# One list of 1788 steps in another order: gated linear attention, then a hard-swish feed-forward, on one core

## The chip, the cores and the metric

The kernel runs on one core of one Trainium2 chip. The metric is the device time of that core in microseconds (us). Before the change the median of three runs is 543.16 us (542.98 to 544.01). A core has a matrix engine (TensorE, PE in the profile, with PEld for its weight loads), a vector engine (VectorE, DVE), a scalar engine (ScalarE, ACT), a general engine (GpSimd, POOL) and a sync engine (SyncE, SP), which here issues all loads and stores. Each engine works through its own queue in the order in which the program gave it instructions.

## The reference

```python
# attention: batch 4, 8 heads, 768 tokens, head size 48
for t in range(S):
    state = alpha[:, :, t, :, None] * state + einsum('bhd,bhe->bhde', k[:, :, t], v[:, :, t])
    y[:, :, t] = einsum('bhd,bhde->bhe', q[:, :, t], state)
# feed-forward on x = y as (3072 tokens, 384)
h = x @ w_in                               # 384 -> 2048
g = h * clip(h + 3.0, 0.0, 6.0) / 6.0
out = g @ w_out                            # 2048 -> 384
```

All inputs come as 64-bit floats[...]; the kernel converts them from their bits.

## The kernel before, in words

The 3072 tokens are 24 tiles of 128 (numbered j); two tiles make a pair g = 0 to 11, and six tiles make one batch entry, where the attention state starts anew. The whole kernel is a set of small functions, one for each kind of step, in a table `steps`. A string lists every step with its numbers, for instance `P.2.3.0`; `run` calls them in that order. The list therefore is the program order on every engine at once: an instruction runs when those ahead of it in its engine's queue have gone and the data and buffers that it needs are ready. The numbers after tile or pair name a bank or a buffer slot.

Steps for one tile of attention:

- `la`, `lk`, `lq`, `lv` load alpha, k, q and v (SP, L251 to L272). From tile 6 on (FIRST = 6) alpha, k and q go into block layouts, whose padding is filled for the first two tiles by a small memset on POOL (L257), issued with the load.
- `ta`, `tk`, `tq` transpose on PE up to tile 5 (L282); from tile 6 on `ca`, `tk`, `tq` are transposes on VectorE (L286). Up to tile 5 `ca` is a ScalarE copy (L300).
- `r` and `p` are two scans on VectorE (L309 with a small reciprocal L313, and L320); `k` and `q` multiply by them (L332).
- `sc`, `u`, `ya`, `yb` are runs of small products on PE (L346 scores, L429 state update, L455 attention output); `m` masks the scores on VectorE (L356); `sm` adds the state (L439), `st` scales it on POOL (L409); `qa`, `sv`, `ck`, `cy` are copies on ScalarE (L366, L419, L378, L464). `cy` gives the feed-forward its input x.
- from tile 8 on `kt`, `kw`, `kr` turn k round by way of DRAM in place of the PE transposes `kb` (L374).

Steps for the weights (16 slices i of 768 KB as they come): `w` loads, `d1`, `d2`, `dx` are ScalarE's part (L186, L196, L191), `d3` VectorE's (two instructions L203, L205 for slices 0, 1, 2, 4; three, L207, L208, L210, for the rest), `d4` an integer add on POOL (L217). Slices 0 to 7 are w_in, 8 to 15 w_out. Raw data stand in three buffers and, for slices 3 and 4, in the part of the second hidden buffer that the steps `fg.1` fill later.

Feed-forward of pairs 0 and 1: `f` (L478), or in halves `fa`, `fb` (L489), is the first layer, `fr` and `fg` its gate (ACT L494, DVE L498); pair 0 has its second layer in `b` (L516). While these use w_in as it is, later pairs use a scheme with fewer multiplications: `y` (25 sums of parts of w_in, made once), `xc` (11 sums of x), 20 products `M` (8 passes, L600), which go out by `n` (ACT copy, L606) and `o` (DVE sums, L537 to L541), then `e` and `h` (gate, L494 and L498). The second layer from pair 1 on is a seven-product scheme: `s` (sums of hidden values, L647 and L664), `P` (16 passes, L703), `K` and `G` (copies and sums of the outputs, L682, L716, L719), `O` (store, L724). `x` are the sums of w_out.

PSUM has eight banks: four for attention, four (m0 to m3) for the feed-forward products, so a product that starts in a bank waits for the last reader of what stood there. `z` (L532) are products with an identity whose results nobody reads; `z.0.8` is eight of them in bank 0.

Of the kernel before, what the change touches and what calls it, by code (L numbers as in the profile page):

```python
# [17 lines left out]
def kernel(  # L18
# [42 lines left out]
    G = 2  # L61
# [510 lines left out]
    for i in range(8):  # L572
        r, o = divmod(i, 3)
        spots.append(raws[r].rearrange("p n w -> p (n w)").bitcast(FP)[:, o * QB : (o + 1) * QB])
    xc = consts.tile([C, len(X_SUMS), C], FP, tag="xc")
# [174 lines left out]
    with tc.manual_schedule():  # L750
        run("""qa.0.0 la.0 z.0.8 ta.0.0 z.0.2 ca.0 lk.0 tk.0.1 la.1 ta.1.2 ca.1 r.0 k.0 kb.0.3 ck.0
               lq.0 tq.0.0 z.0.3 w.2 d1.2 dx.2 p.0 q.0 sc.0.1.2 r.1 m.0 z.0.5 lv.0.0 u.0.3.0 z.0.3
               la.2 ta.2.1 d2.2 ca.2 sv.0.0 lq.1 p.1 tq.1.2 q.1 qa.0.1 qa.1.0 qa.1.1 sm.0.0 lk.1
               tk.1.1 k.1 sc.1.2.3 z.0.1 kb.1.1 r.2 p.2 m.1 sm.0.1 st.1 ck.1 sv.0.1 w.0 d2.0 d1.0
               dx.0 d3.0 d4.0 z.0.2 ya.0.1 yb.0 cy.0 z.0.3 lv.1.1 u.1.2.3 sm.1.0 d3.2 z.0.2 la.3
               lk.2 tk.2.0 k.2 ta.3.2 ca.3 sv.1.0 r.3 d4.2 sm.1.1 st.2 lq.2 tq.2.1 q.2 fa.0.0 sv.1.1
               ya.1.2 kb.2.0 yb.1 sc.2.1.3 w.1 d2.1 d1.1 dx.1 cy.1 fa.2.1 fb.2 d3.1 p.3 m.2 w.3 d2.3
               ck.2 w.5 lk.3 lv.2.2 lq.3 d4.1 w.6 w.7 la.5 fa.1.2 fb.1 lv.3.0 sv.2.0 d2.5 d1.3 d1.5
               fr.0.2.0 d3.3 d3.5 d4.5 u.2.2.0 fb.0 tk.3.1 qa.2.0 fr.0.1.1 ya.2.3 sm.2.0 sm.2.1
               sv.2.1 d4.3 fg.0.2 fg.0.1 st.3 tq.3.2 k.3 q.3 fr.0.0.0 fg.0.0 d2.6 d3.6 f.0.5.3 d1.6  # L760
               d4.6 fr.0.5.1 kb.3.0 ck.3 qa.2.1 sc.3.1.2 m.3 yb.2 d2.7 d3.7 cy.2 qa.3.0 ta.5.0 ca.5
               r.5 sv.3.0 d1.7 d4.7 u.3.1.2 sm.3.0 fg.0.5 f.0.6.1 fr.0.6.0 lk.4 tk.4.3 la.4 ta.4.0
               ca.4 f.0.3.2 sm.3.1 fg.0.6 r.4 st.4 w.9 sv.3.1 d2.9 qa.3.1 ya.3.1 yb.3 cy.3 k.4 p.4
               d1.9 d3.9 d4.9 lq.4 tq.4.2 kb.4.0 f.0.7.0 w.4 d2.4 fr.0.3.1 d3.4 ck.4 f.1.3.3 fg.0.3
               w.8 q.4 sc.4.1.3 p.5 fr.0.7.0 d2.8 d3.8 fg.0.7 d1.4 dx.4 d4.4 d1.8 d4.8 lv.4.1 la.7
               ca.7 u.4.0.2 sm.4.0 m.4 w.12 d2.12 d1.12 d3.12 f.1.0.1 lk.5 d4.12 fr.1.0.1 f.1.7.2
               fr.1.7.0 sv.4.0 fg.1.0 w.10 d2.10 fr.1.3.1 qa.4.0 fg.1.7 tk.5.0 k.5 d1.10 d3.10 d4.10
               la.6 w.11 lk.6 sm.4.1 ca.6 fg.1.3 d2.11 d3.11 d1.11 qa.4.1 d4.11 f.1.6.0 fr.1.6.0
               fg.1.6 tk.6 f.1.1.1 fr.1.1.1 kb.5.1 f.1.5.2 fr.1.5.0 fg.1.5 b.1.0.3 f.1.2.0 w.15
               d2.15 d1.15 lq.5 tq.5.3 r.6 k.6 w.13 lv.5.2 d2.13 fr.1.2.0 d3.15 fg.1.2 d3.13 w.14  # L770
               d1.14 d2.14 lq.6 tq.6 lq.8 fg.1.1 q.5 b.1.1 fa.4.2 ck.5 sv.4.1 fb.4 fr.0.4.0 d1.13
               d4.15 y.3 p.6 y.5 d3.14 fg.0.4 b.0.0.0 b.0.1 sc.5.0.2 u.5.1 st.5 sm.5.0 sv.5.1 m.5
               qa.5.0 qa.5.1 d4.13 lk.8 lv.6.0 sv.6.0 lk.7 q.6 y.6 s.1.1.1 tk.7 f.1.4.1 sv.5.0
               fr.1.4.1 fg.1.4 d4.14 y.10 y.1 x.0 r.7 s.1.0.0 s.1.3.2 y.8 x.1 b.1.2 kb.6.3 ck.6
               P.1.0.2 ya.4.1 ya.5.0 yb.4 yb.5 u.6.2.3 b.0.2 b.1.3 bo.1 cy.4 cy.5 s.1.2.3 x.2 s.1.4
               y.2 k.7 xc.2.1 y.7 p.7 xc.2.3 x.3 xc.2.2 y.9 xc.2.10 y.15 P.1.3.1 K.1.0 P.1.2 K.1.1
               P.1.1.3 G.1.0.0 K.1.2 s.1.5 y.11 P.1.4 G.1.1.1 la.9 la.8 xc.2.4 ca.8 so.1 lq.7 xc.2.5
               y.0 y.4 y.13 P.1.5 b.0.3 bo.0 P.1.6 G.1.3.2 y.12 xc.2.0 y.16 y.17 y.19 y.20 y.18 y.21
               M.2.0.3 qa.6.0 n.2.0.8 xc.2.7 M.2.7.0 n.2.7.9 y.23 xc.2.6 M.2.1 n.2.1.10 sc.6.0.1
               M.2.2 r.8 sm.6.0 tq.7 xc.2.8 qa.6.1 ca.9 q.7 G.1.2.3 la.11 n.2.2.11 sv.6.1 M.2.15.2  # L780
               M.2.16 M.2.3 kb.7.2 M.2.4 n.2.4.12 tk.8 M.2.8 sm.6.1 st.7 m.6 tq.8 o.2.0.0 ya.6.3
               yb.6 sc.7.0.1 M.2.9 xc.2.9 M.2.18.1 o.2.4.0 k.8 y.14 ck.7 qa.7.1 lv.9.1 lv.7.2 sv.7.0
               e.2.0.0 cy.6 qa.7.0 u.7.2.3 o.2.1.0 M.2.10 kt.8 lk.9 n.2.18.13 M.2.17 n.2.10.14
               o.2.6.0 y.22 y.24 sm.7.0 sv.7.1 p.8 h.2.0 M.2.5 M.2.11 n.2.11.15 e.2.4.1 m.7 e.2.1.0
               h.2.1 n.2.5.12 M.2.19 o.2.5.0 M.2.12 n.2.12.11 ya.7.2 yb.7 q.8 o.2.3.0 M.2.6.3 M.2.13
               sc.8.0.1 cy.7 xc.3.1 o.2.3.1 h.2.4 n.2.13.11 o.2.2.0 o.2.7.0 e.2.3.0 o.2.2.1 e.2.2.1
               xc.3.3 sm.7.1 M.2.14 xc.3.4 xc.3.0 xc.3.5 o.2.7.1 P.2.0.1 M.3.0.3 n.3.0.9 xc.3.7
               M.3.7.2 n.3.7.11 h.2.2 xc.3.6 o.2.6.1 h.2.3 xc.3.8 tk.9 e.2.7.1 h.2.7 M.3.1 n.3.1.13
               K.2.0 e.2.6.0 P.2.1.0 M.3.2 kw.8 lv.8.0 O.1.0 O.1.1 la.10 lq.10 lq.9 kr.8 lk.10 O.1.3
               u.8.2.3 ca.10 r.9 qa.8.1 G.2.0.0 k.9 h.2.6 M.3.8 n.3.2.10 e.2.5.1 h.2.5 s.2.0.12  # L790
               s.2.1.15 O.1.2 kt.9 kw.9 M.3.3 M.3.4 n.3.4.8 P.2.3.0 xc.3.9 xc.3.2 o.3.0.0 qa.8.0
               e.3.0.0 M.3.9 M.3.5 s.2.3.14 s.2.2.15 s.2.4 st.8 sv.8.0 K.2.2 o.3.1.0 p.9 xc.3.10
               P.2.2 K.2.1 M.3.10 n.3.10.12 e.3.1.1 s.2.5 P.2.5 tq.9 sm.8.0 sv.8.1 m.8 n.3.5.14 q.9
               qa.9.1 r.10 M.3.11 P.2.4 sm.8.1 h.3.0 st.9 sv.9.0 n.3.11.15 tk.10 G.2.1.1 G.2.2.2
               k.10 kr.9 lq.11 lk.11 sc.9.0.2 m.9 u.9.1.3 h.3.1 sm.9.0 M.3.6.3 kt.10 kw.10 O.2.0
               M.3.12 n.3.12.8 o.3.3.0 ca.11 M.3.18.0 ya.8.0 yb.8 qa.9.0 sv.9.1 n.3.18.10 o.3.6.0
               ya.9.2 yb.9 cy.9 cy.8 M.3.13 n.3.13.8 o.3.3.1 e.3.3.0 o.3.2.0 xc.4.1 o.3.2.1 o.3.7.0
# [135 lines left out]
```

## Time and profile before

| | |
|---|---|
| median of 3 runs | 543.16 us |
| profiled execution: time, span | 543.03 us, 541.3 us |
| PE busy, records | 525.4 us, 6306 |
| VectorE busy | 482.3 us |
| ScalarE busy | 258.5 us |
| POOL busy | 50.1 us |
| HBM read, written | 44.50 MB, 8.91 MB |

The span runs from the first to the last instruction of the profiled execution; its own time lies 1.7 us above. Each fp32 product appears as two records on PE ("passes"); a transpose as one. In the groups "L703 PE" means the matmuls that line 703 of the kernel issues. Busy time of PE is modelled from the starts of the matmuls, so a full row of nines says that no long hole is there, not that a matmul could not be closer to the next.

### The profile page before, as it was taken

Reading aid. Unit: us, or ns where it says so; the run is one execution under the profiler, and the core shown is the slowest. Engines: PE = TensorE matmul, PEld = TensorE weight load, DVE = VectorE, ACT = ScalarE, POOL = GpSimd, SP = SyncE. Lnnn points to the kernel's source line nnn. Section 1 sums busy time; section 2 is a strip of 40 time slices with the busy share of each in tenths; the row PEclk is TensorE's granted clock in tenths of the full one; section 3 lists DMA queues with packets and bytes.
Section 4 is the critical chain, followed back from the end, with each engine's and each line's share of the span. In section 5 each row is a group of like instructions: output and inputs, shape, how many; then the busy total and the mean of one; then the engine's idle time right before and its main releaser. Section 6 shows DMA issues by size and latency. Waiting matters only on the chain.

```text
span 541.3 us, 15109 instructions
## 1 busy us (share of the span) xinstructions
PE 525.4 (97%) x6306; PEld 499.0 (92%) x6306; DVE 482.3 (89%) x849; ACT 258.5 (48%) x503; POOL 50.1 (9%) x71
## 2 busy tenths in 40 slices
PE   8799889899999999999999999999999999999996
PEld 7698767788999999999999999999999999999996
DVE  7999889999999999999999999999999989686381
ACT  4898845311654544453543653643444544443330
POOL 5252424100000000000000000000000000000000
PEclk9999999999999999999999999999999999999999
DMA  9998864410462246355165225352453151000101
GB/s 182 229 245 235 211 208 121 116 42 1 90 157 55 74 104 132 95 124 123 39 149 127 68 69 122 78 136 70 88 127 92 22 127 34 21 9 15 37 9 36
DMA packets 124100, 54.40 MB, mean 101 GB/s; under 512 B 83328, under 2 KB 116864, under 8 KB 124032
## 3 DMA queue, kind: packets, MB, share of 16 engines
q1 hardware_dynamic: 124032, 53.44, 41.4%
q8 instruction: 49, 0.80, 0.6%
q14 instruction: 19, 0.16, 0.1%
HBM read 44.50 MB, written 8.91 MB: 99 GB/s over the span
## 4 chain that ended last, share of the span: by engine, by line
PE 87%; DVE 6%; issue 2%; DMA 2%; ACT 2%; POOL 1%; DVEq 0%; POOLq 0%; ACTq 0%; SPq 0%
PE m_ps L703 36%; PE m_ps L600 34%; PE t_ps L455 4%; PE m_ps L516 3%; PE t_ps L429 2%; PE m_ps L489 2%; PE t_ps L346 2%; PE m_ps L478 1%; PE m_ps L532 1%; POOL w L217 1%; DVE R L309 1%; DMA raw<-in_moe_w_out_dram 1%; DMA kq<-in_k_dram 1%; PE t_ps L282 1%; DVE w L537 0%
## 5 line engine op out<-in xcount | busy, mean ns | idle before, releaser
L703 PE MATMUL m_ps<-w,g_sb 128*128 128x192 f32 x704 | 121.5, 326 | 0.0
L606 ACT COPY g_sb<-m_ps 128x512 f32<-128x512 f32 x110 | 63.8, 584 | 114.9 <-PE m_ps L600 109.4
L703 PEld LDWEIGHTS m_ps<-w,g_sb 128*128 128x128 f32 x704 | 113.8, 190 | 0.3
L703 PE MATMUL m_ps<-rings,g_sb 128*128 128x192 f32 x528 | 91.5, 327 | 0.0
L703 PEld LDWEIGHTS m_ps<-rings,g_sb 128*128 128x128 f32 x528 | 85.4, 190 | 0.4
L600 PE MATMUL m_ps<-xc,w 128*128 128x128 f32 x640 | 84.3, 278 | 0.2 <-DVE xc L537 0.2
L600 PEld LDWEIGHTS m_ps<-xc,w 128*128 128x128 f32 x640 | 78.0, 192 | 1.7 <-issue 0.3
L494 ACT ACTIVATE r<-g_sb,half 128x512 f32<-128x512 f32 x80 | 57.2, 723 | 44.1 <-DVE g_sb L541 18.5
L498 DVE SCALAR_TENSOR_TENSOR g_sb<-r,g_sb 128x512 f32<-128x512 f32 x80 | 53.9, 681 | 2.8 <-ACT r L494 2.2
L600 PE MATMUL m_ps<-xT,raw 128*128 128x128 f32 x400 | 51.6, 276 | 0.1
L600 PEld LDWEIGHTS m_ps<-xT,raw 128*128 128x128 f32 x400 | 48.4, 192 | 0.5 <-ACT g_sb L606 0.2
L409 POOL TENSOR_TENSOR st<-sm,R 128x192 f32<-128x192 f32 x20 | 13.1, 654 | 358.8 <-DVE sm L439 297.7
L647 DVE TENSOR_TENSOR g_sb<-g_sb 128x512 f32<-128x512 f32 (+1 forms) x55 | 42.1, 789 | 3.5 <-PE m_ps L703 3.2
L600 PE MATMUL m_ps<-xT,w 128*128 128x128 f32 x320 | 42.0, 275 | 0.0
L366 ACT COPY A<-q 48x256 f32<-48x256 f32 x88 | 35.4, 403 | 8.9 <-DVE q L332 7.7
L600 PEld LDWEIGHTS m_ps<-xT,w 128*128 128x128 f32 x320 | 39.4, 192 | 0.1
L356 DVE TENSOR_TENSOR A<-t_ps,mask 64x256 f32<-64x256 f32 x96 | 36.0, 413 | 0.5
L478 PE MATMUL m_ps<-xT,w 128*128 128x256 f32 x144 | 33.1, 382 | 1.1 <-DVE g_sb L498 1.1
L537 DVE TENSOR_TENSOR g_sb<-g_sb 128x512 f32<-128x512 f32 x40 | 27.2, 691 | 6.9 <-ACT g_sb L606 6.2
L309 DVE TENSOR_TENSOR_SCAN R<-t,ones 128x516 f32<-128x516 f32 x24 | 30.4, 1265 | 2.6 <-ACT t L300 2.6
L600 PE MATMUL m_ps<-xc,raw 128*128 128x128 f32 x240 | 32.0, 276 | 0.0
L478 PEld LDWEIGHTS m_ps<-xT,w 128*128 128x128 f32 x144 | 26.6, 190 | 5.2 <-DVE g_sb L498 1.8
(104 smaller groups left out, 735.5 us busy)
## 6 DMA issues: line engine op xcount, KB each, us to landing
raw<-in_moe_w_out_dram SPq DMA_DIRECT2D x8, 768.0 KB, 4.5
raw<-in_moe_w_in_dram SPq DMA_DIRECT2D x6, 768.0 KB, 6.7
v<-in_v_dram SPq DMA_DIRECT2D x48, 96.0 KB, 3.2
out_dram<-oh SPq DMA_DIRECT2D x44, 96.0 KB, 1.8
far<-kq SPq DMA_DIRECT2D x64, 64.0 KB, 2.2
kb<-far SPq DMA_DIRECT2D x64, 64.0 KB, 2.0
aq<-in_alpha_dram SPq DMA_DIRECT2D x36, 96.0 KB, 2.5
kq<-in_k_dram SPq DMA_DIRECT2D x36, 96.0 KB, 2.6
```

The costliest lines, as they stand in the source:

```text
L309: nc.vector.tensor_tensor_scan(out=reverse(R, n - 1, n), data0=reverse(ax, n, n), data1=reverse(ones, n, n), initial=0.0, op0=ALU.mult, op ...
L356: nc.vector.tensor_tensor(out=to[:, a], in0=sc[a][half], in1=mask[half, half].unsqueeze(1).to_broadcast([HB, NP, HB]), op=ALU.mult)
L366: nc.scalar.copy(out=to[:, a], in_=Q_t[j][64 * a : 64 * a + D, :, half])
L455: nc.tensor.matmul(y_of(j, (i + 1) // 2, p)[:, HB * b : HB * b + HB], vb[:, p, e : e + 32], A_t[j][:, b, 2 * p + a], start=(b == 0 and i = ...
L478: nc.tensor.matmul(h[:, f], w1[:, kk, o : o + C], xT_t[g][:, kk], start=(kk == 0), stop=(kk == KT - 1))
L494: nc.scalar.activation(out=to, in_=h, func=AF.Relu, bias=half, scale=1.0 / 6.0)
L498: nc.vector.scalar_tensor_tensor(out=to, in0=r, scalar=1.0, in1=h, op0=ALU.min, op1=ALU.mult)
L537: eng.tensor_tensor(out=out, in0=in0, in1=in1, op=ALU.add if s1 > 0 else ALU.subtract)
L600: nc.tensor.matmul(acc[g][i][:, f * C : (f + 1) * C], spots[w][:, f * C : (f + 1) * C], x_of(g, x), start=(first and f == 0), stop=last, s ...
L606: nc.scalar.copy(out=slots[z], in_=acc[g][i])
L647: nc.vector.tensor_tensor(out=out, in0=in0, in1=in1, op=ALU.subtract)
L703: nc.tensor.matmul(to[g], a, rhs[:, f], start=(first and f == 0), stop=(last and f == HF - 1), skip_group_check=True)
```

## The change

The string is replaced by another order of the same steps. No function changes, and the number of steps of each kind for each tile, pair and slice is the same, 1788 in all. What differs is where each step stands, and which bank or slot it uses; the `z` steps are still 29 products in sum, of which three now stand in pair 2's part. Among pair 0's half steps, `fa` and `fb` keep their work and change banks. The core of the diff, with the places that the prediction speaks of:

```diff
-        run("""qa.0.0 la.0 z.0.8 ta.0.0 z.0.2 ca.0 lk.0 tk.0.1 la.1 ta.1.2 ca.1 r.0 k.0 kb.0.3 ck.0
-               lq.0 tq.0.0 z.0.3 w.2 d1.2 dx.2 p.0 q.0 sc.0.1.2 r.1 m.0 z.0.5 lv.0.0 u.0.3.0 z.0.3
...
-               ya.1.2 kb.2.0 yb.1 sc.2.1.3 w.1 d2.1 d1.1 dx.1 cy.1 fa.2.1 fb.2 d3.1 p.3 m.2 w.3 d2.3
...
-               w.8 q.4 sc.4.1.3 p.5 fr.0.7.0 d2.8 d3.8 fg.0.7 d1.4 dx.4 d4.4 d1.8 d4.8 lv.4.1 la.7
-               ca.7 u.4.0.2 sm.4.0 m.4 w.12 d2.12 d1.12 d3.12 f.1.0.1 lk.5 d4.12 fr.1.0.1 f.1.7.2
-               fr.1.7.0 sv.4.0 fg.1.0 w.10 d2.10 fr.1.3.1 qa.4.0 fg.1.7 tk.5.0 k.5 d1.10 d3.10 d4.10
-               la.6 w.11 lk.6 sm.4.1 ca.6 fg.1.3 d2.11 d3.11 d1.11 qa.4.1 d4.11 f.1.6.0 fr.1.6.0
-               fg.1.6 tk.6 f.1.1.1 fr.1.1.1 kb.5.1 f.1.5.2 fr.1.5.0 fg.1.5 b.1.0.3 f.1.2.0 w.15
...
-               M.2.0.3 qa.6.0 n.2.0.8 xc.2.7 M.2.7.0 n.2.7.9 y.23 xc.2.6 M.2.1 n.2.1.10 sc.6.0.1
...
-               P.11.1.3 K.11.2 K.11.1 P.11.4 s.11.5 P.11.5 O.9.2 so.0 O.9.3 G.11.1.1 O.11.1 P.11.6
-               G.11.3.2 O.11.3 O.10.3 G.11.2.0 O.11.2 G.11.0.1 O.11.0""")
+        run("""z.0.5 z.0.3 z.0.1 z.0.8 qa.0.0 w.0 d2.0 d3.0 la.0 ta.0.0 ca.0 r.0 lk.0 tk.0.1 k.0
+               z.0.2 p.0 la.1 ta.1.2 lq.0 tq.0.3 ca.1 r.1 lk.1 lv.0.0 sv.0.0 d1.0 kb.0.0 ck.0 z.0.2
+               u.0.2.1 sm.0.0 sv.0.1 q.0 qa.0.1 tk.1.0 k.1 p.1 z.0.2 sc.0.2.3 m.0 la.2 ta.2.0 ca.2
+               dx.0 w.2 d2.2 kb.1.0 ck.1 lq.1 r.2 sm.0.1 st.1 tq.1.2 q.1 d3.2 z.0.3 d1.2 dx.2 lv.1.1
...
+               qa.1.0 d2.3 ya.1.2 yb.1 cy.1 fa.1.2 lq.3 ck.2 d1.3 p.3 d3.3 lv.2.2 u.2.3.2 sm.2.0
+               d4.3 fb.2 tq.3.1 q.3 fb.1 qa.2.0 sm.2.1 sv.2.0 st.3 fr.0.2.0 fg.0.2 lk.4 tk.4.0
...
+               fr.0.6.1 yb.2 cy.2 w.9 d2.9 q.4 qa.4.1 d1.4 d1.9 dx.4 la.6 w.8 d3.4 r.5 lk.5 w.10
+               d3.9 p.5 ca.6 fg.0.6 d4.9 w.12 lq.5 lv.4.1 d2.8 d3.8 f.0.7.2 d1.8 st.4 d4.8 d4.4 w.11
+               fr.0.7.0 fg.0.7 f.1.7.0 fr.1.7.1 fg.1.7 sc.4.0.2 m.4 f.1.1.1 fr.1.1.0 fg.1.1 f.1.3.3
+               fr.1.3.1 d2.10 d1.10 tk.5.3 f.1.0.2 d2.12 d3.10 d4.10 w.13 fg.1.3 fr.1.0.0 fg.1.0 k.5
...
+               d4.13 sc.5.0.3 yb.4 f.1.5.0 fr.1.5.1 fg.1.5 tk.6 m.5 b.1.0.2 fb.4 b.1.1 d1.15 d4.15
+               st.5 y.5 w.14 la.7 lk.7 cy.4 d2.14 qa.5.1 ck.5 b.0.0.1 fr.0.4.0 d3.14 k.6 q.6 ca.7
...
+               y.19 xc.2.6 sm.6.0 G.1.2.2 y.20 M.2.0.2 lv.12.1 la.8 O.1.1 O.1.0 ca.8 y.18 y.21 y.23
...
+               st.7 lk.8 O.1.3 lq.8 lk.9 la.9 la.10 tk.8 tq.8 lq.10 lq.9 ya.6.1 yb.6 M.2.9 z.1.3
...
+               e.11.2.0 h.11.2 s.11.4 e.11.3.1 h.11.3 P.11.1.0 s.11.5 G.11.0.1 O.11.0 O.10.3 K.11.1
+               P.11.4 G.11.1.2 P.11.5 G.11.2.1 O.11.2 P.11.6 G.11.3.0 O.11.3 O.9.2 O.11.1""")
```

## The prediction

> **What bounds the kernel now.** I read the page first, then busy time by stage, then the waits, then the order of time at the places that the new order changes.
>
> ```profile
> span 541.3 us, 15109 instructions
> PE 525.4 (97%) x6306; PEld 499.0 (92%) x6306; DVE 482.3 (89%) x849; ACT 258.5 (48%) x503; POOL 50.1 (9%) x71
> PE   8799889899999999999999999999999999999996
> DMA  9998864410462246355165225352453151000101
> ```
>
> TensorE is busy nearly throughout; only the first ten slices (13.5 us each) and the last show holes. Loads fill the DMA engines in the first five slices. By stage (columns: stretch, its length, then busy us and instructions of each engine, clock, DMA share, GB/s):
>
> ```profile
> 0.00:27.00 27.00, 21.42 (x310) 19.10 (x310) 22.41 (x42) 17.27 (x27) 10.91 (x23) 1.00 1.03 206
> 27.00:54.00 27.00, 26.51 (x458) 23.16 (x457) 26.28 (x44) 23.91 (x41) 11.10 (x9) 1.00 0.93 239
> 54.00:81.00 27.00, 23.16 (x163) 18.43 (x162) 23.31 (x34) 17.84 (x27) 9.15 (x12) 1.00 0.77 211
> 81.00:108.00 27.00, 25.73 (x307) 19.80 (x307) 26.65 (x38) 12.13 (x22) 7.88 (x12) 1.00 0.47 119
> 108.00:135.00 27.00, 26.64 (x150) 23.19 (x149) 26.01 (x42) 3.98 (x10) 0.00 (x0) 1.00 0.08 22
> 135.00:459.00 324.00, 323.90 (x4215) 318.13 (x4214) 310.16 (x568) 155.64 (x324) 11.01 (x17) 1.00 0.41 96
> 459.00:541.30 82.30, 77.98 (x713) 77.18 (x711) 47.44 (x87) 27.73 (x55) 0.00 (x0) 0.99 0.07 21
> ```
>
> From 135 us on PE idles 0.1 us in 324. VectorE is close behind (310 of 324, 13.8 idle): two engines run neck and neck, and a product often starts 0.1 to 0.5 us after the vector result that it needs. So the time is PE's fixed work, plus its stalls up to 132 us (where M.2.0, the first fast product, starts), plus the tail. In starts of neighbouring matmuls, taking the commonest distance of each kind as its rate, PE loses 17.0 us before M.2.0 and 2.9 after. What ends waits there:
>
> ```profile
> DVE t L286 <- POOL aq L257: 3.2, 2, 1.8
> PEld t_ps L282 <- DVE s L439: 2.3, 2, 2.0
> PEld m_ps L478 <- DVE g_sb L498: 1.8, 2, 1.5
> ```
>
> The first is the root of the others: VectorE's transposes of alpha for tiles 7 and 6 (ca.7, ca.6) waited 1.42 and 1.75 us for a small fill on POOL that stood in POOL's queue behind the weight adds d4.8 and d4.10. Behind each transpose in VectorE's queue stood results that PE needed (sm.4.0, fg.1.3). A second loss is in the same stage, VectorE beside POOL:
>
> ```profile
> 61.21 2.49 DVE L210 SCALAR_TENSOR_TENSOR raw<-raw,w 128x768 uint32<-128x768 uint32 x1
> 69.64 0.96 DVE L210 SCALAR_TENSOR_TENSOR raw<-raw,w 128x768 uint32<-128x768 uint32 x1
> 60.68 2.20 POOL L217 TENSOR_TENSOR w<-w,g_sb 128x768 int32<-128x768 int32 x1 [3.56 <-ACT g_sb L191]
> ```
>
> The same instruction takes 0.96 us alone and 2.49 beside a POOL add.
>
> **What the Trainium skill says.** TensorE: Matmul & The Clock Gate, section "Architectural detail": the vector, scalar and POOL queues are strict FIFO, and only TensorE may pull a weight load ahead. The trace agrees: the fills above waited for their turn. The same page, Part 3, "The mechanism": a weight load overlaps a running matmul only where its row group differs. That fits the stops below. GPSIMD Engine Reference, section 1: POOL shares its SBUF interfaces with VectorE; the 2.49 against 0.96 us is that. DMA: Bandwidth & Descriptors, "Issuing engines are not separate DMA queues": all loads share 16 engines; here landings before 45 us follow each other at some 1.15 us per 192 KB tile and 2.0 to 2.3 us per weight slice.
>
> **The change, part by part.** No step is added or dropped; both orders hold 1788 steps, the same products and the same 29 idle ones (58 records). Only places, banks and slots move, so the costs are in stalls.
>
> *Stops of small-product runs.* In order of time on PE:
>
> ```profile
> 152.68 1.16 PE L600 MATMUL m_ps<-xc,w 128*128 128x128 f32 x8
> 153.68 1.06 PE L600 MATMUL m_ps<-xc,raw 128*128 128x128 f32 x8
> 154.66 0.69 PE L346 MATMUL t_ps<-q,k 48*64 48x64 f32 x32
> 155.41 1.16 PE L600 MATMUL m_ps<-xc,w 128*128 128x128 f32 x8
> ```
>
> A pass of L600 normally starts 0.112 us after the last. Into a small run it takes 0.205, out of it 0.149 where a small pass takes 0.007, and one load later costs 0.101: 0.093+0.142+0.101 = 0.34 us per run. Counting the two orders, 45 runs become 43, and changes of kind inside runs go from 51 to 53 at 0.03 each: -0.68+0.06 = **-0.6 us**.
>
> *Tail.* After PE's last product:
>
> ```profile
> 537.02 0.32 ACT L716 COPY oh<-m_ps 128x192 f32<-128x192 f32 x1 [10.08 <-PE m_ps L703]
> 537.36 1.77 SPq L724 DMA_DIRECT2D out_dram<-oh  x4
> ```
>
> SP issues four stores behind the last copy, 0.47 us apart (O.11.3, O.10.3, O.11.2, O.11.0). The new order leaves three (O.11.3, O.9.2, O.11.1). The end follows the last issue, so **-0.5 us**.
>
> *The start.* SP's first load is now weight slice 0, then alpha, k, alpha, q. Alpha of tile 0 landed at 4.0 us; one slice ahead of it makes that about 6.2. PE first does 17 idle products (34 records; at the cold 0.213 us until 6.6 us, then 0.112) to about 7.8, so the first scan r.0 moves from 6.75 to about 9.1. Meanwhile VectorE converts slice 0 (d3.0, 1.3 us), formerly done at 21 us. VectorE loses 2.3-1.3 = 1.0, and gains 0.4 where q.1 used to wait for its load: **+0.5 us** on VectorE. If the slice comes too late to be that cover, it is +2.3. Behind the new first load stand all the other loads; by my count of landings la.5 comes at 41.9, as before (41.8).
>
> *The two fills.* la.6 now stands before d4.9 in the list, so its fill follows d4.7 on POOL, with ca.6 some 9 us of vector work behind d3.7. la.7's fill follows d4.15 and st.5, with 8 us of vector work from d3.15 to ca.7. Both waits should go: -3.2 us on VectorE. SP must have passed w.9 for la.6 and w.14 for la.7, by my walk at 47 and 82 us, 10 us or more before they are needed. VectorE's waits for G.1.0 and G.1.1 (0.8 together) go too, since these now stand later than their products: -0.8. Sum on VectorE: -3.2-0.8+0.5 = **-3.5 us**. The overlap of vector conversions with POOL adds also changes; it stretched VectorE by some 6 us in all (means against commonest distances on L203 to L210 and the scans). I take no change, with -2 and +2 as ends.
>
> *What of this reaches PE.* For each product I sum PE's work ahead of it and VectorE's work up to the result it needs, at the commonest distances (scan 1.26+0.10, second scan 1.14, multiply 0.60, mask 4 x 0.36, transpose 0.96, xc sum 0.22; PE: M 0.90, P 2.60, f 2.60). The difference is the lead; PE's stalls must be at least VectorE's lateness minus the lead. Before, the least leads are 1.9 (f.1.1.1), 2.5 (b.1.0), 3.9 (M.2.7: 116.5-112.6), 4.1 (P.2.3: 151.8-147.7). These are the very places where PE waited or had no slack. After: 1.1 (f.1.3), 1.5 (f.1.0), 2.9 (b.1.0), 4.5 (M.2.1: 117.2-112.7), 3.6 (P.2.3: 150.3-146.7). VectorE's lateness at P.2.3 was 21.3 and becomes 21.3-3.5 = 17.8, so PE's stalls there can fall from 16.9 to 17.8-3.6 = 14.2: -2.7. My walk along PE itself (loads, conversions, then banks freed by fg steps) puts M.2.0 at 127.9 instead of 131.9, -4.0, so P.2.3 binds. Later the least lead at tile pair 8 falls from 20.0 to 17.6 (P.8.1). Without recovery only -0.9 would be left; VectorE has 13.8 us of idle in 135 to 459 to recover from, so I give back 0.5: **-2.2 us**. The three idle products now in M.2 are inside these sums.
>
> Sum: -0.6-0.5-2.2 = -3.3. The profiled execution took 543.03 (1.7 around its span), so 539.7; the median of the runs shown is 0.1 higher, giving **539.8**.
>
> **Rivals.** *Gain lost in the middle*: VectorE, at 96% there, can't recover, or its conversions overlap POOL more (+2), and PE stalls in M.2 to P.8. What is left is stops and tail, -1.1: 542.1. For it: the smaller leads at P.2.3 and P.8.1. Against: the 13.8 us of idle. *Late start carried through* (slower): ScalarE is 24 of 27 us busy in 27 to 54. The 2.3 us of the first alpha would then pass unabsorbed through its queue, and cy.1, which lets fb.2 start, stands behind more copies (29.8 becomes 31.3 by my walk, +1.5). That gives 3.8-1.1 = +2.7: 545.9. It decides once more than 2.2 us of the delay reaches M.2.0. Against: the same walk has PE at f.0.3 at 39.0 with as much work behind it (29.5 us) as before at f.0.5. *All of the opening*: VectorE's -3.5 and better overlap (-2) reach PE, so -5.5-0.6-0.5 gives 536.6. Against: P.2.3's lead. That the order is changed but not the critical queue is ruled out for the fills, which do move.
>
> **How the numbers follow.** Forecast 0.48 (own range 538.5 to 541.2); gain lost 0.17, half of it within 0.2% (1.1 us, about what a measurement can tell); late start 0.22, nearly all of it slower; whole opening 0.08; other gains lost by a single new wait of about 1 us 0.05. Faster 0.48+0.08+0.08+0.05 = 0.69, same 0.10, slower 0.21. The range 537.2 to 545.2 leaves about one in ten on each side.
>
> **What would show it.** No wait of DVE L286 on POOL; r.0 at 9 us; M.2.0 at 128 to 129 us; three stores after the last copy; 43 small runs; PE without a wait over 0.5 us at P.2.3. Wrong if ScalarE's cy.1 comes after 33 us, if f.1.x waits for banks in sum more than 4 us, or if PE stops behind vector sums at pair 8.

## The result, and the profile after

The kernel after takes 536.38 us (median of 4 executions, 536.24 to 537.02), the kernel before 543.20 (4 executions, 542.98 to 544.01): a ratio of 0.9874, 95% interval 0.9857 to 0.9891, 6.8 us less. The forecast was 539.8 with a range of 537.2 to 545.2. It had the sign right and the time just outside its range, at the fast end: 3.4 us less were forecast, twice as much came. M.2.0, foretold for 128 to 129 us, starts at 125.70. The profiled execution took 536.33 us with a span of 534.5.

Where the two traces part can be read from three marks:

| | before | after | difference |
|---|---|---|---|
| start of M.2.0, the first fast product | 131.88 us | 125.70 us | -6.18 |
| from there to the last matmul's start | 404.78 | 404.71 | -0.07 |
| from there to the end of the span | 4.59 | 4.12 | -0.48 |

So nearly all of it lies ahead of M.2.0. The page of the kernel after, in the lines that answer to those shown of before:

```profile
span 534.5 us, 15145 instructions
PE 524.2 (98%) x6306; PEld 498.9 (93%) x6306; DVE 477.1 (89%) x849; ACT 257.6 (48%) x503; POOL 50.4 (9%) x71
PE   7799999999999999999999999999999999999997
DMA  9998877006615155254354455055364042100001
```

VectorE was busy 482.3 us and now is 477.1, with the same 849 instructions: some of them take less time. By stage (stretch, its length, then busy us and instructions of PE, PE's loads, VectorE, ScalarE and POOL, granted clock, DMA share, GB/s):

```profile
27.00:54.00 27.00, 26.77 (x437) 23.95 (x434) 26.44 (x44) 24.96 (x49) 8.94 (x9) 1.00 0.98 259
54.00:81.00 27.00, 27.00 (x282) 23.26 (x281) 25.08 (x41) 20.45 (x31) 10.91 (x9) 1.00 0.77 204
81.00:108.00 27.00, 27.00 (x187) 19.23 (x186) 26.73 (x35) 9.96 (x21) 7.48 (x14) 1.00 0.37 86
135.00:459.00 324.00, 324.00 (x4173) 318.48 (x4172) 308.93 (x565) 152.60 (x319) 10.19 (x17) 1.00 0.41 95
```

In 54 to 108 us PE was busy 48.89 of 54 us; now it is busy 54.00. In starts of neighbouring matmuls, counted as in the prediction, PE loses 10.15 us up to 45 us in the kernel before and 10.10 in the kernel after, so nothing is gained up to there; up to M.2.0 it loses 17.00 and 10.84. What the change gains ahead of M.2.0 is gained between 45 us and M.2.0. VectorE's waits in the first 135 us:

```profile
DVE w L203 <- ACT w L196: 2.4, 1, 2.4
DVE s L439 <- PE t_ps L429: 1.3, 1, 1.3
DVE half L80 <- PEq L915: 0.8, 1, 0.8
```

The line with L286 behind POOL, 3.2 us before, is gone from this list. The first of these is the new start: VectorE waits for the first weight slice. Conversions beside POOL adds, from the order of time:

```profile
59.62 0.69 DVE L207 TENSOR_SCALAR w<-w 128x768 f32<-128x768 f32 x1
60.95 0.96 DVE L210 SCALAR_TENSOR_TENSOR raw<-raw,w 128x768 uint32<-128x768 uint32 x1
...
81.70 2.03 POOL L217 TENSOR_TENSOR w<-raw 128x768 int32<-128x768 int32 x1 [0.17 <-POOL kq L257]
82.38 1.77 DVE L207 TENSOR_SCALAR w<-w 128x768 f32<-128x768 f32 x1
92.69 1.96 DVE L332 TENSOR_TENSOR q<-q,P 128x512 f32<-128x512 f32 x1
```

The same L207 takes 0.69 or 1.77 us. Against the lower quartile of each form, instructions stretched in this way before 132 us lost 5.9 us in the kernel before and 3.8 in the kernel after. At the end:

```profile
530.77 0.32 ACT L716 COPY oh<-m_ps 128x192 f32<-128x192 f32 x1 [10.08 <-PE m_ps L703]
528.61 3.79 SPq L724 DMA_DIRECT2D out_dram<-oh  x4
```

Three of these four stores stand behind the last copy, as forecast.

### The profile page after: what moved, and what is told of

It reads as the page before. It is cut to its first block, busy times and chain, and to the rows that moved or that the text cites. A ratio compares the mean times of both kernels' runs of the same rounds, so it can differ in the third digit from the quotient of the medians.

```text
span 534.5 us, 15145 instructions
## 1 busy us (share of the span) xinstructions
PE 524.2 (98%) x6306; PEld 498.9 (93%) x6306; DVE 477.1 (89%) x849; ACT 257.6 (48%) x503; POOL 50.4 (9%) x71
## 4 chain that ended last, share of the span: by engine, by line
PE 88%; DVE 6%; POOL 2%; ACT 1%; DMA 1%; issue 0%; SPq 0%; DVEq 0%; POOLq 0%
PE m_ps L703 34%; PE m_ps L600 34%; PE m_ps L478 6%; PE t_ps L455 4%; PE t_ps L346 2%; PE t_ps L429 2%; PE m_ps L489 2%; DMA v<-in_v_dram 1%; PE m_ps L516 1%; DVE rings L647 1%; PE t_ps L282 1%; DVE raw L537 1%; ACT raw L191 1%; DVE g_sb L647 1%; DVE w L537 1%; POOL v L96 1%
## 5 line engine op out<-in xcount | busy, mean ns | idle before, releaser
L600 PE MATMUL m_ps<-xc,w 128*128 128x128 f32 x640 | 82.7, 277 | 0.3 <-DVE w L541 0.3
L600 PEld LDWEIGHTS m_ps<-xc,w 128*128 128x128 f32 x640 | 77.5, 192 | 1.5 <-issue 0.5
L600 PE MATMUL m_ps<-xT,raw 128*128 128x128 f32 x400 | 52.5, 277 | 0.0
L600 PEld LDWEIGHTS m_ps<-xT,raw 128*128 128x128 f32 x400 | 48.6, 192 | 0.6
L600 PE MATMUL m_ps<-xT,w 128*128 128x128 f32 x320 | 42.0, 276 | 0.0
L600 PEld LDWEIGHTS m_ps<-xT,w 128*128 128x128 f32 x320 | 39.3, 192 | 0.1
L600 PE MATMUL m_ps<-xc,raw 128*128 128x128 f32 x240 | 31.8, 276 | 0.0
L600 PEld LDWEIGHTS m_ps<-xc,raw 128*128 128x128 f32 x240 | 29.6, 192 | 0.1
```

Of the source, the lines that this page charges most:

```text
L600: nc.tensor.matmul(acc[g][i][:, f * C : (f + 1) * C], spots[w][:, f * C : (f + 1) * C], x_of(g, x), start=(first and f == 0), stop=last, s ...
```

## The experiments

Two theories stood at first. A: PE's stalls before M.2.0 follow VectorE's lateness, which two things make: the waits for the alpha fills, and instructions that take longer beside a POOL add (their stretch). B: they follow the order and the banks of PE's own products, and VectorE is not the cause. A third cause came to light on the way and is told with its runs. The kernels for these runs are those of before or after with the one edit shown. The runs share the busy time of 62 to 108 us as a measure (columns as above), here before and after:

```profile
62.00:108.00 46.00, 40.96 (x374) 31.47 (x374) 42.19 (x62) 22.82 (x39) 14.19 (x22) 1.00 0.58 160
```

```profile
62.00:108.00 46.00, 46.00 (x402) 35.69 (x401) 44.04 (x64) 23.41 (x41) 15.75 (x20) 1.00 0.56 142
```

### The fills, in both directions

In the kernel before, the fills of alpha tiles 6 and 7 were taken out of the load and issued on POOL ahead of d4.6:

```diff
-        if j < FIRST + NQ:
+        if j < FIRST + NQ and name != "a":
...
+    def pad_a(j):
+        for o in (BLK, 3 * BLK):
+            nc.gpsimd.memset(quads["a", j % NQ][o : o + BLK, :, V - 1, D - BLK : BLK], 1.0)
...
-  d2.6 d3.6 f.0.5.3 d1.6 d4.6
+  d2.6 d3.6 f.0.5.3 d1.6 pa.7 pa.6 d4.6
```

> The kernel before with one edit: the two small POOL fills for alpha of tiles 7 and 6 are issued ahead of the weight add d4.6 instead of behind d4.8 and d4.10; everything else keeps its place. Theory A (the opening was lost by VectorE being late, and these fills are the largest part): the two waits of 3.2 us are gone from VectorE, PE's stalls before M.2.0 fall from 17.0 to some 14, time 540.2 (539.5 to 541). Theory B (the places of the first-layer products and their banks decide, the fills are hidden behind them): 542.5 to 543.4.

Measured: 539.85 us (5 executions, 539.44 to 540.14), ratio 0.9942 (0.9922 to 0.9961) against 542.87. M.2.0 starts at 128.62 us, 3.26 earlier; no wait of L286 on POOL is left.

```profile
62.00:108.00 46.00, 43.71 (x390) 33.71 (x389) 45.25 (x66) 22.81 (x39) 14.07 (x18) 1.00 0.59 161
```

PE's busy time in the stage grows by 2.75 us without any product of PE having been moved. The reverse, in the kernel after: the same fills put behind POOL adds, with the transposes right behind them.

```diff
-  d3.14 k.6 q.6 ca.7 fg.0.4 d1.14 d4.14
+  d1.14 d3.14 d4.14 pa.7 ca.7 k.6 q.6 fg.0.4
...
-  d3.9 p.5 ca.6 fg.0.6
+  d3.9 p.5 fg.0.6
...
-  st.4 d4.8 d4.4
+  st.4 d4.8 pa.6 ca.6 d4.4
```

> The changed kernel with the fills put back behind weight adds: fill of tile 6 behind d4.8 with its transpose ca.6 right behind d3.8, fill of tile 7 behind d4.14 with ca.7 right behind d3.14, which makes VectorE wait as in the kernel before. Theory A: VectorE waits some 1.9 and 1.8 us for POOL; 1.3 of it takes the place of its wait for the tile-4 state update at 70 us, the rest reaches PE: 538.0 (537.2 to 539). Theory B: below 536.9.

Measured (one execution): 538.79 us, span 537.0, M.2.0 at 127.97. The wait is back, and PE's stalls with it:

```profile
DVE t L290 <- POOL aq L267: 4.1, 2, 2.1
```

```profile
62.00:108.00 46.00, 44.37 (x376) 34.27 (x377) 41.32 (x63) 22.51 (x39) 15.47 (x22) 1.00 0.55 141
```

(L290 is line 286 of the kernel after, moved by the added lines.) VectorE waits 4.1 us, of which 2.27 reach M.2.0. B, which had the fills without influence, falls as the only cause.

### The POOL adds cut to 8 columns, in both kernels

This leaves out the low bits of the weights, and with them nearly all of POOL's work in this stage; everything else keeps its place.

```diff
-        nc.gpsimd.tensor_tensor(out=dst.bitcast(I32), in0=high.bitcast(I32),
-                                in1=lo.bitcast(I32), op=ALU.add)
+        nc.gpsimd.tensor_tensor(out=dst[:, 0:1, 0:8].bitcast(I32),
+                                in0=high[:, 0:1, 0:8].bitcast(I32),
+                                in1=lo[:, 0:1, 0:8].bitcast(I32), op=ALU.add)
```

> The kernel before with POOL's weight adds d4 cut to 8 columns of each slice, so the low weight bits are left out for the rest: POOL is nearly free, so neither the overlap with VectorE (5.9 us of stretched vector instructions before 135 us) nor the fills' wait (3.2 us) is left. Theory A: nearly all of the opening's difference goes, about 537.0 (536 to 538.5). Theory B: the order of the products still costs, 540 or more.

> The changed kernel with the same cut adds (low weight bits left out). Its VectorE is stretched by 3.8 us in the opening, but PE has no stall from 45 us to M.2.0, so little can be gained there. Theory A: 535.8 (535.2 to 536.4), so that the difference to the kernel before with cut adds is 1 to 2 us, of which 0.5 tail and 0.6 stops. Theory B: the difference stays at 4 us or more.

Measured (one execution each): before 538.01 us, M.2.0 at 126.84; after 535.73, M.2.0 at 125.55.

```profile
62.00:108.00 46.00, 45.08 (x395) 34.95 (x394) 44.72 (x67) 22.44 (x39) 6.26 (x20) 1.00 0.58 153
```

```profile
62.00:108.00 46.00, 46.00 (x401) 35.63 (x400) 42.92 (x66) 23.15 (x41) 4.94 (x18) 1.00 0.51 126
```

With the adds out of the way the two kernels are 2.3 us apart instead of 6.8; theory A had expected 1 to 2. The times of these single executions need care. In that of the kernel before the granted clock was 0.5 from 18.1 to 21.5 us, and it stands 0.24 us behind the one with early fills at 41 us, where both have issued the same products. By stage, with the clock as the third column from the right:

```profile
15.00:20.00 5.00, 3.13 (x45) 2.86 (x46) 3.56 (x7) 2.09 (x6) 0.00 (x0) 0.81 0.93 157
20.00:25.00 5.00, 5.00 (x117) 4.34 (x116) 4.63 (x11) 4.89 (x7) 0.54 (x2) 0.85 1.01 310
```

So the comparison is taken from 41 us to M.2.0: 87.89 us with early fills, 85.87 with small adds, which is 2.02 less. VectorE's instructions that are stretched by over 0.2 us lose 5.2 us before 132 us with early fills and 0.5 with small adds. In the kernel after, the small adds bring 0.15 at M.2.0, 0.14 of it ahead of 41 us: what stretch is left there is covered. Between the two kernels 1.3 us remain at M.2.0 (126.84 against 125.55), which neither the fills nor POOL explain.

### What remains: a stop inside a run of small products

Lengths of runs and places in them are counted here in passes, from 0; a product is two passes. (The expectations call a pass a product: their runs of 128 and 160 are passes too.)

In the trace of the kernel with small adds PE stands still once in that stage, inside a run of small products, for 1.13 us. The kernel before has the same stop. It was in its list of waits, and the prediction passed it over:

```profile
PE t_ps L429 <- issue: 1.4, 1, 1.4
```

```profile
104.15 1.99 PE L455 MATMUL t_ps<-A,v 128*32 128x64 f32 x128
106.07 0.66 PE L429 MATMUL t_ps<-v,kb 64*64 64x48 f32 x26
108.18 0.33 PE L429 MATMUL t_ps<-v,kb 64*64 64x48 f32 x6 [1.44 <-issue]
108.43 1.88 PE L516 MATMUL m_ps<-w,g_sb 128*128 128x384 f32 x5
```

"issue" is time in which the engine waits for nothing that the profile shows. The run ya.4 ya.5 yb.4 yb.5 u.6 has 160 passes, the only one so long; it stops behind pass 153, and 1.66 us lie between the starts of this pass and the next, where 0.015 is usual. The longest run of the new order has 128. So a theory Q: a long run stops PE. Its first run, with VectorE's sums moved behind the update that they read:

```diff
-  u.13.0.2 sc.13.1.3 M.5.12 P.4.4
+  sc.13.1.3 M.5.12 P.4.4
...
-  ya.12.3 yb.12 cy.12 yb.13 cy.13
+  ya.12.3 yb.12 cy.12 yb.13 u.13.0.2 sm.13.0 cy.13
...
-  ya.14.2 yb.14 sv.15.1 yb.15 cy.15
+  ya.14.2 yb.14 sv.15.1 yb.15 u.15.0.3 sm.15.0 sm.15.1 cy.15
```

> The kernel after with the state updates u.13 and u.15 (and the VectorE sums that read them) moved from ahead of two large products to the end of the run of small products that follows, so that two runs of 128 become runs of 160; the number of runs stays 43. Theory Q (a run of small products longer than some 150 stops PE for over 1 us, wherever it stands): at about the 154th product of each of the two runs PE stops for 1.1 to 1.7 us without a wait that the profile shows; time 536.4 + 2 x 1.1 to 1.7 = 538.6 to 539.8. Rival L (the stop in the kernel before belongs to its place: loads, or a wait for an operand): no such stop, 536.2 to 536.8.

Measured: 539.6 us (538.64 to 539.61, 3 executions). In this kernel the copies sv.13.1 and sv.15.1 take the half state before its sum, so that part of the attention result is of an older state; instructions and sizes are the same. Of the two runs of 160 only u.13's stopped, behind its pass 150 and for 1.18 us; u.15's did not. A miss for both sides: the stop can be made anew, but length alone does not make it.

The same run cut in the kernel before, by moving u.6 behind the next large product, once with the small adds, once with the early fills, and once with nothing else:

```diff
-  yb.4 yb.5 u.6.2.3 b.0.2 b.1.3
+  yb.4 yb.5 b.0.2 u.6.2.3 b.1.3
```

> The kernel before with the POOL adds of the weights cut to 8 columns, as in the run with small adds (the conversion of the weights is left incomplete by it), and with the one run of 160 small products cut into 128 and 32 by the large product behind it (b.0.2). Theory Q: the stop of 1.13 us at 102 us goes, a further run costs 0.34: M.2.0 at 126.1 instead of 126.8, time 537.2. Rival L: the stop stays at u.6, M.2.0 at 126.8 to 127.2, time 538.0 to 538.4.

> The kernel before with the two fills of alpha early, as in the first experiment, and with the run of 160 small products cut by b.0.2. Theory Q, with PE not held by VectorE any more: 539.85 - 1.2 + 0.34 = 539.0, M.2.0 at 127.8. If VectorE's lateness holds PE there instead (it was 3.6 us less covered before), the stop goes but another wait takes its place: 539.6 to 539.9.

> The kernel before with its one run of 160 small products cut into 128 and 32 by the large product behind it, and nothing else. Theory Q: the stop of 1.66 us inside the run goes and a further run costs 0.34. If that reaches the end beside the fills' waits: M.2.0 at 130.6, time 541.9. If VectorE's lateness (21.3 us at P.2.3, stalls 17.0, lead used 4.3 of about 5) holds PE instead: at most 0.7 of it is left, 542.5 or more. Rival L: the stop stays, 543.2.

Measured. With small adds: 535.49 us (2 executions), M.2.0 at 124.22, the stop gone, PE busy 46.00 of 46. M.2.0 is 2.62 us earlier than without the cut, which is more than Q expected. But 1.59 of it stand before 41 us, where the two programs are alike: the execution without the cut is the one with the clock of 0.5 from 18.1 to 21.5 us. From 41 us to M.2.0 it is 1.0 us, near the 0.8 forecast. With adds and stop gone, and the fills' waits down to 0.6 us, the kernel before is at 535.49 us and the kernel after with small adds (one execution) at 535.73: nothing of the 6.8 us is left. With early fills: 538.61 us (11 executions, 537.32 to 541.33), M.2.0 at 127.50, 1.12 earlier than with the fills alone. With nothing else: 541.94 us (20 executions, 541.58 to 542.98), ratio 0.9984 (0.9977 to 0.9991), M.2.0 at 130.32, 1.57 earlier. The stop goes in all three. In the kernel before it had not reached the end in full: of the 1.57 us, 0.34 are lost again behind M.2.0 (405.12 us to the last matmul's start instead of 404.78, with the wait of L600 for xc grown from 0.2 to 0.5 us), and the medians differ by 0.95.

The first two of these three also measure the stretch a second time: with early fills and the run cut it is 86.77 us from 41 us to M.2.0, with small adds and the run cut 84.84, which is 1.93 less. So from 41 us to M.2.0 the runs of the kernel before bring 3.26 by the fills, 1.12 by the cut and 1.93 by the adds, 6.3 us in all; the kernel after gains 6.1 between 45 us and M.2.0, and cutting its adds brings 0.01 there. (Up to 41 us the execution with small adds and the cut is 1.35 us ahead of the one with early fills and the cut. Of this 0.5 stand ahead of any add; whether the rest is the adds' is open.)

Length or place? Six long runs at once (four of 160, two of 144 passes), made as above in the kernel after, with other slots where a run's own stand in the way:

> The kernel after with the state updates u.9, u.13, u.15, u.17, u.19 and u.23 (and the VectorE sums that read them) moved to the end of the run of small products that follows: four runs of 160 and two of 144 in place of six of 128. Some copies of the state then come before the sum that they should follow, so the attention result is of an older state; the instructions and their sizes are the same. Theory Q in the form that the runs so far leave (a run that passes some 150 small products is liable to stop PE for over 1 us, not every time): stops of about 1.1 us without a shown wait in at least two of the four runs of 160, near product 150; none in the two of 144 or in the remaining runs of 128. Rival L (the stop is tied to its place in the program): only u.13 stops again.

Measured: 539.3 us (538.99 to 539.5, 3 executions). Only u.13's run stopped, behind pass 150 again (1.41 us):

```profile
264.69 1.99 PE L455 MATMUL t_ps<-A,v 128*32 128x64 f32 x128
266.61 0.56 PE L429 MATMUL t_ps<-v,kb 64*64 64x48 f32 x23
268.36 0.34 PE L429 MATMUL t_ps<-v,kb 64*64 64x48 f32 x9 [1.19 <-issue]
```

Q as I had it falls, and rival L, "the place decides", took this run. What is there at the place? In the two traces a transfer of one kind alone runs during the stop, here in the kernel before, 104 to 109 us:

```profile
q8 instruction: 1, 0.02, 1.8%
```

Over the whole kernel this queue carries 49 packets of 16 KB, 0.80 MB. By their number these are PE's own instructions. The Trainium skill, Runtime: NRT & Kernel Launch, section "Instruction fetch mechanics", says that instructions come in blocks of 16 KiB, 256 instructions, and that crossing a block is "mostly hidden". The trace agrees on the blocks: 6306 passes with a load each over 49 blocks are 129 passes per block. It shows a case that is not hidden. The middle half of the fetches in the kernel before come 98 to 149 passes after the one ahead. Around the stop the distances are 200 and 75: one fetch, at 105.39 us, comes about 80 passes late (at 0.015 us each, some 1.2 us), and its packet ends at 106.81; PE stops at 106.5 and goes on at 108.2. The same pair is there at u.13's run (199 and 86). In all six stopped runs of the traces PE goes on 1.25 to 1.48 us after the end of such a packet.

A late fetch alone does not stop PE: in the kernel before the fetches at 188.06 and 478.54 us, beside runs of 128, come 191 and 218 passes after the one ahead, and nothing stops. Theory F: a run of small products goes through a whole block in 2 us; where a block begins early enough in the run to be used up inside it, PE stands before the next one. By my count back from the fetches, that means a beginning in the first 17 or so of 160 passes, so that a run of 128 can't stop at all. Two runs test it by leaving out eight idle products at the very start, which shifts every block by 16 passes against runs that are not touched:

```diff
-        run("""z.0.5 z.0.3 z.0.1 z.0.8 qa.0.0 w.0
+        run("""z.0.5 z.0.3 z.0.1 qa.0.0 w.0
```

> The kernel with six long runs of small products once more, with eight idle products fewer at its very start, which moves every later instruction of PE 16 records nearer to the front of its stream. (As before, some copies of the state come before the sum that they should follow.) Theory F (PE's instructions come in blocks of 16 KB; a run stops where it uses up a whole block before the next has come, which needs a block to begin in the first 17 or so of its 160 products; in the run before this, blocks begin at product 7 of u.13's run, which stopped at 150, and 6 and 5 products ahead of u.15's and u.19's runs, which did not): all blocks begin 16 products later, so u.13's run stops no more, and u.15's and u.19's runs stop at about product 153, for 1.1 to 1.7 us each. Rival L (the stop belongs to u.13's place or operands): u.13's run stops again, u.15's and u.19's don't.

> The kernel before with eight idle products fewer at its very start, and nothing else. Theory F: the block that began at product 10 of the run of 160 now begins at 26, so that the run ends before it is used up: the stop of 1.66 us goes, no further run is made, M.2.0 at about 130.2, time 541.5 to 542.0. Rival L: the stop stays, M.2.0 at 131.9, time 543.0 to 543.4.

Measured, six long runs (539.96 us, 2 executions): u.13's run no longer stops (0.45 us are left in the large product behind it), and u.19's, which had not stopped before, stops behind pass 151 for 1.85 us. u.15's run, for which I had expected a stop too, has none.

```profile
264.65 1.99 PE L455 MATMUL t_ps<-A,v 128*32 128x64 f32 x128
266.57 0.68 PE L429 MATMUL t_ps<-v,kb 64*64 64x48 f32 x32
...
384.50 1.99 PE L455 MATMUL t_ps<-A,v 128*32 128x64 f32 x128
386.42 0.56 PE L429 MATMUL t_ps<-v,kb 64*64 64x48 f32 x24
388.62 0.33 PE L429 MATMUL t_ps<-v,kb 64*64 64x48 f32 x8 [1.64 <-issue]
```

The kernel before with the same shift: 541.68 us (12 executions, 541.04 to 542.76), ratio 0.9978 (0.9969 to 0.9986), M.2.0 at 129.90, 1.98 earlier. Of this 0.62 stand ahead of 41 us already, where PE has eight products less to do. Its run of 160 stands uncut and no longer stops:

```profile
103.58 1.99 PE L455 MATMUL t_ps<-A,v 128*32 128x64 f32 x128
105.50 0.68 PE L429 MATMUL t_ps<-v,kb 64*64 64x48 f32 x32
```

F holds in three of its four points (before, u.13, u.19) and L falls. A count that needs no fetch says the same: from PE's first pass on, u.13's stop is ahead of pass 3265 in both kernels with long runs, and with eight products left out the 0.45 us in the large product are ahead of pass 3265 too, 16 passes further on in the program. The stop keeps its place in PE's stream, not in the list of steps. At u.15's run the fetch came with pass 9 of the run and was in time; at u.19's it came with pass 126. Why one fetch comes so much later than another stays open, and with it the fourth point.

### The terms of the sum, one by one

The tail. In the kernel after, O.11.1 was moved ahead of O.11.2 and O.9.2 ahead of O.11.0:

```diff
-  G.11.0.1 O.11.0 O.10.3 K.11.1 P.11.4 G.11.1.2 P.11.5 G.11.2.1 O.11.2 P.11.6 G.11.3.0 O.11.3 O.9.2 O.11.1
+  G.11.0.1 O.9.2 O.11.0 O.10.3 K.11.1 P.11.4 G.11.1.2 P.11.5 G.11.2.1 O.11.1 O.11.2 P.11.6 G.11.3.0 O.11.3
```

> The kernel after with two of its last three stores (O.11.1 and O.9.2) issued before O.11.2 and O.11.0, so that only one store is left behind the last copy. Theory A (the end follows the last issue on SP, 0.47 us per store): span shorter by 0.94 us, 533.6, and a time of 535.4. Rival T (the end follows the last store's landing, however many stand before it): span 534.5, time 536.4 as it was.

Measured: 535.28 us (535.20 to 535.36), span 533.6. The span is 0.93 us shorter. SP issues two stores in this last stretch where there were four:

```profile
528.64 2.83 SPq L724 DMA_DIRECT2D out_dram<-oh  x2
```

The price of 0.47 us per store behind the last copy is right, and rival T falls.

The start:

```diff
-        run("""z.0.5 z.0.3 z.0.1 z.0.8 qa.0.0 w.0 d2.0 d3.0 la.0 ta.0.0 ca.0 r.0 lk.0 tk.0.1 k.0
-               z.0.2 p.0 la.1 ta.1.2 lq.0 tq.0.3 ca.1 r.1
+        run("""qa.0.0 la.0 z.0.8 ta.0.0 ca.0 r.0 lk.0 tk.0.1 k.0
+               z.0.2 p.0 la.1 ta.1.2 lq.0 w.0 tq.0.3 ca.1 r.1 d2.0 d3.0
```

> The kernel after with alpha, k, alpha and q loaded ahead of weight slice 0, as before, and with slice 0's conversion moved behind r.1; nine idle products are spread over the first gaps as before. It tests the term 'start' of the sum. Theory A (VectorE's work ahead of M.2.0 sets PE, and the new start costs it 0.5 us): M.2.0 comes 0 to 0.8 us earlier, time 535.6 to 536.4. Rival S (the new start is itself a part of the unforeseen gain, slice 0 being converted while VectorE has nothing else): M.2.0 at least 1 us later, time 537.4 or more.

Measured: 535.96 us (535.82 to 536.11), M.2.0 at 125.27, 0.43 earlier. So the new start costs what was put down for it (0.5); other moves ahead of 45 us have made up for it, since PE's loss up to there is the same in both kernels.

The idle products in pair 2:

```diff
-  M.2.9 z.1.3 M.2.18.1
+  M.2.9 M.2.18.1
```

> The kernel after without the three idle products that stand behind M.2.9 (0.67 us of PE; they compute nothing that is used). If PE's own work sets the time from M.2.0 on: -0.67 us, 535.7. If VectorE's lead at the products that follow (M.2.14, P.2.3) is used up, so that the idle products only fill a wait: 0, 536.4, with a new PE stall of 0.4 to 0.7 us there. Theory A holds VectorE 15.9 us late at P.2.3 against stalls of 10.9 and a lead of 3.6, so it expects most of it lost: 536.1 (535.7 to 536.4).

Measured: 536.50 us (536.27 to 536.74), span 534.5: nothing is gained, where theory A had expected 0.3. PE has a new wait at that very place, for VectorE's sum:

```profile
138.50 0.68 DVE L541 SCALAR_TENSOR_TENSOR g_sb<-m_ps,g_sb 128x512 f32<-128x512 f32 x1
139.23 0.60 PE L600 MATMUL m_ps<-xc,w 128*128 128x128 f32 x3 [0.41 <-DVE g_sb L541]
```

In the kernel after the three idle products stand there instead:

```profile
137.80 0.83 PE L532 MATMUL m_ps<-ident 128*128 128x128 f32 x6
```

The stops at the edges of small runs: eleven large products moved into runs, of the kind

```diff
-  kw.14 kr.14 u.14.1.2 M.6.3 M.6.4
+  M.6.3 kw.14 kr.14 u.14.1.2 M.6.4
```

(that is, M.6.3 now stands between sc.14 and u.14).

> The kernel after with eleven of its runs of small products cut in two by a large product that stood beside them, so that 43 runs become 54 and changes of kind inside runs fall by 11. By the terms of the sum, 11 x (0.34 - 0.03) = 3.4 us: 539.8, all of it in PE after 135 us and none of it before (M.2.0 at 125.7). Rival: VectorE, close behind PE there, sets the time as much as PE does and the stops are hidden in its waits: under 1 us, 537.0 or less.

Measured: 540.40 us (540.09 to 541.24, 6 executions). In the profiled execution PE's clock was 0.96 in the first 45 us, which puts M.2.0 at 126.44; from there to the last matmul's start it takes 408.51 instead of 404.71, 3.8 us for eleven runs, or 0.35 per run net (the changes of kind inside runs fell from 25 to 6 there; with 0.03 for each, 0.40). So PE sets the time over this stretch, though not at every place (at 139 us it was VectorE, as shown above), and the price of 0.34 was, if anything, a little low.

### A version that beats both

The two edits that helped, the start and the tail, together:

> The kernel after with both edits that helped alone: the attention loads ahead of weight slice 0, and one store instead of three behind the last copy. If their gains add: -0.4 at M.2.0 (125.3) and -0.94 at the end, span 533.1, time 534.9 to 535.1. If the two share a cause they would not add: 535.3 or more. Against the kernel before: ratio 0.985 to 0.9855.

Measured: 534.90 us (5 executions, 534.82 to 535.16), ratio to the kernel before 0.9836 (0.9812 to 0.9861). The gains add, and this is the fastest version that was run.

## Why the prediction was right in its sign and wrong in its size

**Right.** No wait of L286 on POOL; r.0 at 8.7 us (9 foretold); three stores behind the last copy, -0.5; the start +0.5 (measured +0.43; its own parts, 1.0 less 0.4, make 0.6); from 135 us on PE's fixed work (no wait of PE beyond a few tenths); the fills' term itself, 3.2 on VectorE, of which the run with early fills alone brought 3.26 at M.2.0. None of the three signs of a wrong prediction came: cy.1 stood at 31.9 us, no product of f.1 waited for a bank, PE did not stop at pair 8. What happened is nearest to the rival called "all of the opening" (536.6), which I gave 0.08. That its number is met within 0.2 us is in part luck: it has 5.5 us from the fills, the G waits and the overlap, and nothing of the stop.

**Wrong.** The term "what of this reaches PE" was 2.2 us; it measured 6.2. The runs give its parts: the fills 3.3, the long run's stop 1.1 (on top of the fills), and the stretch beside POOL 1.9. The first two are told by M.2.0, the third from 41 us to M.2.0, in the kernel before; in the kernel after cutting the adds brings 0.01 there, so the new order avoids or covers all of it. The sum is 6.3 of the 6.1 us that were gained between 45 us and M.2.0. It rests on single profiled executions, and what is left (0.2) is too small to be told by them. The greatest failure was the overlap put at nothing, then the stop that was passed over. Four steps failed:

1. *The lead at P.2.3 as a hard limit.* I let only 2.7 of VectorE's 3.5 us through, by taking the lead up to the start of P.2.3. But the product is 16 passes, and its first eight read only the sum s.2.0. In the order of time after:

```profile
159.85 0.69 DVE L664 TENSOR_TENSOR g_sb<-g_sb 128x512 f32<-128x512 f32 x1
161.56 2.77 PE L703 MATMUL m_ps<-w,g_sb 128*128 128x192 f32 x16
161.93 0.68 DVE L664 TENSOR_TENSOR g_sb<-g_sb 128x512 f32<-128x512 f32 x1
```

   P.2.3 starts 0.4 us before its second sum does. Eight passes at 0.163 are 1.3 us more of lead, 4.9 instead of 3.6. VectorE was 15.9 us late there and PE had lost 10.9, a lead in use of 5.0. The figures of the kernel before said so too: 21.3 late with stalls of 16.9 is 4.4 in use, where I had put the limit at 4.1. With the eight passes that limit is 5.4. Limit and all, the walk along PE (127.9) and this sum (129 or so) were both too late.

2. *The overlap of VectorE with POOL, "I take no change, with -2 and +2 as ends".* On VectorE it came out at -2.1 by the traces, the end of its bound, and the runs put 1.9 of M.2.0's gain down to it. The order of the adds against the conversions could have been laid out in time before the result, as the walk did for the loads; I had bounded it instead.

3. *The give-back of 0.5 at pair 8.* PE lost 2.9 us after M.2.0 in both kernels, so nothing was given back. VectorE was 35.4 us late at P.8.1 before and 27.7 after. Less PE's own losses (at most 19.9 and 13.7), some 15.5 of the lead of 20.0 were in use before and 14.0 of 17.6 after: the smaller lead did not bind. (Without recovery 3.5 less 2.4 would have left 1.1, not 0.9.)

4. *The waits for G.1.0 and G.1.1, 0.8.* The gain was right in size, the reason not. I booked VectorE as waiting for products because it asked too early. The products were late, because PE had stood 1.7 us in the run of 160 just ahead. "PE t_ps L429 <- issue: 1.4" was the line that said so. With the run cut and nothing else, VectorE's two waits are gone from its list and M.2.0 comes 1.57 us earlier.

One term was too large: *the stops*, -0.6. The runs fell from 45 to 43 as counted, but the changes of kind inside runs rose from 25 to 33, not from 51 to 53 (I had counted like beside like as a change). With the prices of the prediction that is -0.44 in all, and -0.53 from M.2.0 on, where 30 runs became 28 and 20 changes 25. Measured from M.2.0 on: three idle products came in (0.67 us), 32 small passes went out (0.49), and the time from there to the last matmul's start fell by 0.07, which leaves about 0.25. The idle products in part fill a wait, as the run without them showed, so this remainder is not firm. The price held in the run with eleven more stops; the count was wrong.

In sum: -2.2 forecast to M.2.0 became -6.2 by 0.8 (the lead), 0.5 (the give-back), 1.9 (the overlap), some 0.3 (the stop, beyond the 0.8 booked for the G waits) and 0.5 (the start, which other moves made up for); the stops gave 0.5 less. That is about the 3.4 us between forecast and result.

## What to carry to other kernels

Take a lead to the pass that reads the late operand, not to the start of its product, and lay an engine's work beside POOL out in time instead of bounding it. At an "issue" wait in the middle of a run of short instructions, look at the instruction queue; here it went when the run was cut to 128 passes, or when the instructions ahead of it were shifted. Where two engines run neck and neck, a loss ahead of the tight stretch counts as long as the other engine's lead lasts, so undo the suspected losses one at a time and read where the first fast product starts. Before two single executions are compared, look at the granted clock of each and at a mark that both have passed with the same work.

## What the runs showed of the hardware that I had not expected

- PE stopped for 1.1 to 1.9 us inside runs of 160 small passes (0.015 us each), behind pass 150 to 153, in six of the fourteen such runs in all traces. It went on 1.25 to 1.48 us after a fetch of a block of its instructions had ended. Leaving out eight idle products 100 to 385 us earlier moved the stop from one run to another. In no trace did a run of 144 passes or fewer stop so after 45 us. That the block ran out there is the theory that fits best; one run that it has stopping did not stop.
- Beside a POOL add, VectorE's L332 on two SBUF tiles took 1.96 us instead of 0.68 and L207 1.77 instead of 0.69, and POOL's add took 2.03 or 2.17 instead of 1.47. The Trainium skill, GPSIMD Engine Reference, section 1, names the shared interfaces; the size is from here.
- A full-size product between small ones costs 0.35 to 0.40 us. TensorEngine Tiling (Array Packing), section "Key Properties", says that a change of tiling mode drains TensorE; that agrees, and gives no price.
- With the same program up to 41 us, two executions stood 1.6 us apart there, the later one with a granted clock of 0.5 from 18.1 to 21.5 us. Four executions of the kernel before and of its variants with whole adds and the same start agree there within 0.02 us.
